# Attention and gated feed-forward on one core: bias tiles of head pairs two to four loaded ahead, first input split one step later

## The chip, the core and the metric

The kernel runs on one core of one Trainium2 chip. The metric is the device time of one execution in microseconds (us); lower is better. Several executions are timed and their median counts; one more execution is recorded by the hardware profiler, and all durations below come from that one.

The core has five engines with an instruction stream each: PE (matrix multiplies, with its weight loads shown apart as PEld), DVE (vector work), ACT (activations and copies), POOL (GpSimd, vector work here), and SP, which in this kernel only issues DMA transfers. The streams run on their own and wait for each other through semaphores.

## What is computed

```
scores = q k^T / 8 + bias[h, i, j]            # 4 batches, 8 heads, 576 x 576
bias   = relu(x[i, j] * w1 + b1) @ w2         # x = log1p(|i - j|) / log1p(max(i, 1)), hidden size 32
attn   = exp(scores - max) / sum
y      = attn v                               # to 4 x 576 x 512
h      = relu(y @ w_in)                       # 512 -> 1024
c      = three-tap convolution of h along the sequence
out    = (h * sigmoid(c)) @ w_out             # 1024 -> 512
```

The bias depends on the head and on the position, not on the batch. It is therefore computed once, written to device memory, and read back for each pair of heads.

## The kernel before

The program has three stages. The first computes the bias with small matrix multiplies and writes its rows to a buffer `bias_d` in device memory through five staging tiles; one of the staging tiles (`st34`) lives in the pool `raw_p`, which has two buffers of 9,728 bytes per partition. Attention starts underneath, and is the second stage. The third stage is the feed-forward network, batch after batch.

Attention is cut into 16 sequence steps `n`, each one pair of heads `p` of one batch `b`, in the order `seq = [(p, b) ...]`: pair 0 has `n` 0 to 3, pair 1 has 4 to 7, pair 2 has 8 to 11 and pair 3 has 12 to 15. A step has five units `t`: unit 0 holds the first 64 query rows of both heads, units 1 to 4 hold 128 rows of each head. The order is written out by hand: the list `flat` of 77 units, and one loop over it. In the iteration of unit `u` stand

- the score matrix multiplies (L350) of unit `u + 2` and their evaluation on DVE (`reduce`, L361): one instruction for each head, which adds the bias tile to the scores and takes the row's extreme;
- the exponentials (`expo`, L375, ACT) of unit `u + 1`;
- the transposes of unit `u` (L409, L421) and their copies on DVE and ACT (L91, L88);
- a few products with `v` (L458), which stand in the queue `fill`;
- a step of the preparation of the feed-forward weights (L97 and L103 on DVE, L99 on ACT, L131 and L132 on POOL).

`reduce` for unit `(n, t)` reads the bias tile `biast[p, t]`. A tile is 128 rows of both heads, 576 KB in two DMAs of 288 KB (L177); unit 0 has a smaller one (L179). The pool `bias_p` holds four tiles, one for each of `t` = 1 to 4, and `bias0_p` one for `t` = 0. The four batches of a pair use the same five tiles. The tiles of pair `p + 1` are loaded in the last batch of pair `p`: right behind the evaluation of unit `(n, t)`, which was the last to read the tile of pair `p`, its buffer is filled anew,

```
if b2 == B - 1 and p2 + 1 < NP:
    load_bias(p2 + 1, t2)
```

and read one step, five units, later. All these transfers stand in SP's stream, in the order in which the program issues them, among the queries and keys of step `n + 2` (L151, L152), the values of step `n + 1` (L166 to L169), the weights (L118), and the row sums' way through device memory (L484 to L486 and L491). The DMAs of SP count on eight semaphores in turn, and one that reuses a semaphore waits until the DMA before it on that semaphore has landed.

At the end of attention the result of batch 0 is split into two parts for the feed-forward multiplies: `x_parts(0, c)` for the four chunks `c`, two instructions each on POOL (L131, L132). Two chunks share one tile `xs` of the pool `raw_p`. Chunks 0, 1 and 2 stand in step 14 at units 2, 3 and 4, chunk 3 in step 15 at unit 0. The feed-forward multiplies of batch 0 (L523) begin in step 15 at unit 3. POOL also multiplies by the inverse sums (`apply_norm`, L498) in the same stream. When the four splits are done, a buffer of `x_p` becomes free, and the last weight rows (`raw_o`) are loaded into it.

Of the kernel before, what the change touches and what calls it, by code (L numbers as in the profile page):

```python
# [9 lines left out]
F32 = mybir.dt.float32  # L10
# [9 lines left out]
def attention_ffn_kernel(  # L20
# [12 lines left out]
    B, S, DM = out.shape  # L33
    NP = qk.shape[1]
# [4 lines left out]
    P = 128  # L39
# [19 lines left out]
    def pool(stack, name, bufs, **kw):  # L59
        return stack.enter_context(tc.tile_pool(name=name, bufs=bufs, reuse_waits="tile", **kw))  # L60
# [7 lines left out]
    raw_p = pool(ctx, "raw", 2)  # L68
# [15 lines left out]
    NSEQ = len(seq)  # L84
# [45 lines left out]
    def split_x(dst, x):  # L130
        first = nc.gpsimd.tensor_scalar(dst[:, 0], x, 1.0, 0.0, op0=ALU.mult, op1=ALU.add)  # L131
        nc.gpsimd.tensor_sub(dst[:, 1], x, dst[:, 0].bitcast(F32))  # L132
        return first

    with tc.manual_schedule():
# [3 lines left out]
        bias_p = pool(att, "bias", 4)  # L139
        bias0_p = pool(att, "bias0", 1)  # L140

        vts, qks, sms, biast = {}, {}, {}, {}


        def load(n):
# [23 lines left out]
            nc.sync.dma_start(vt[TL:P, 9], v[b, p, TL:P, 4])  # L169

        def load_bias(p, t):
            bt = bias_p.tile([P, 2, S], F32, name="bt") if t else bias0_p.tile([P, 1, S], F32, name="bt0")
            for h in range(2):
                c = (2 * p + h) * BW
                if t:
                    i0 = TL + (t - 1) * P
                    nc.sync.dma_start(bt[:, h], bias_rows[i0:i0 + P, c:c + S])  # L177
                else:
                    nc.sync.dma_start(bt[TL * h:TL * h + TL, 0, :], bias_rows[0:TL, c:c + S])  # L179
            biast[p, t] = bt  # L180
# [146 lines left out]
        def turned_sp(n, t):  # L327
            tile = sp_p.tile([P, 2 * S + 2], F32R, name="sr", tag=spt[n, t][1])
            nc.scalar.activation(tile[:, 2 * S:], pars[:, 0:2], AF.Copy)
            spt[n, t] = (tile, None)  # L330
# [28 lines left out]
        def reduce(ps, n, t, h):  # L359
            bt = biast[seq[n][0], t]  # L360
            nc.vector.tensor_tensor_reduce(  # L361
                out=halves(spt[n, t][0][:, h]),
                in0=ps[:, :, 0:HS],
                in1=halves(bt[:, h]),
                op0=ALU.add,
                op1=ALU.min,
                scale=-scale,
                scalar=3.0e38,
                accum_out=nms[n, t][:, h:h + 1],
            )  # L370

        def expo(n, t, h):
            sp, nm = spt[n, t][0], nms[n, t]
            col = 4 * h + t - 1 if t else 8
            exps[n, t, h] = nc.scalar.activation(  # L375
                sp[:, h], sp[:, h], AF.Exp, bias=nm[:, h:h + 1], scale=-1.0,
                accum_out=sms[n][:, col:col + 1],
            )
# [92 lines left out]
        def invert(n):  # L471
            sm, r = sms.pop(n), rr_t[n % 2][:, 0:9]
            nc.vector.tensor_scalar(r, sm, 1e-9, None, op0=ALU.add)
            nc.vector.reciprocal(r, r)
# [20 lines left out]
        def apply_norm(n):  # L495
            p, b = seq[n]
            assert waiting[n] == 0
            nc.gpsimd.tensor_mul(xb[b][:, p], xb[b][:, p], rbs.pop(n))  # L498
# [7 lines left out]
        def x_parts(b, c):  # L506
            if c % 2 == 0:
                xss["raw"] = raw_p.tile([P, 2, 2, S], F32R, name="xs", tag="raw")
            xs = xss["raw"][:, c % 2]
            first = split_x(xs, xb[b][:, c])  # L510
            if b == 1 and c == 0:
                tc.add_manual_dep(first.ins, gated[0, FC - 2].ins.name, mybir.DependencyInfo(
                    mybir.DependencyClass.Sync, mybir.DependencyReason.DATA))
            xss[b, c] = xs
# [57 lines left out]
        def heads(t):  # L572
            return (0, 1) if t else (0,)
# [25 lines left out]
        for i in range(NBLK):  # L599
# [18 lines left out]
            if fill:  # L618
                fill.popleft()()
        bias_out(*last)  # L620
        load_bias(0, 4)
        while fill:
            fill.popleft()()
        for _ in unit:
            pass
        for u in range(2):
            for h in heads(flat[u][1]):
                reduce(scores(*flat[u], h), *flat[u], h)
            if u == 0:
                for h in heads(flat[0][1]):  # L630
                    expo(*flat[0], h)
                turned_sp(*flat[0])
        pv_share = (2, 2, 1, 3, 2)
        hs_ff = {}
        raw_w = {}
# [4 lines left out]
        for u, (n, t) in enumerate(flat):  # L640
            p, b = seq[n]
            ui = units.index(t)
# [48 lines left out]
            if u + 2 < NU:  # L691
                n2, t2 = flat[u + 2]
                p2, b2 = seq[n2]
                if b2 == B - 1 and p2 + 1 < NP:
                    load_bias(p2 + 1, t2)
            if ui == (0 if n > 1 else 1) and n > 0:
                invert(n - 1)
            if ui == (2 if n > 1 else 3) and 1 <= n and n + 1 < NSEQ:
# [7 lines left out]

            if ui == 2 and n > 1:
                apply_norm(n - 2)
            if n == NSEQ - 2 and ui > 1:
                x_parts(0, ui - 2)  # L710
            if n == NSEQ - 1 and ui == 0:
                x_parts(0, 3)
            if n == NSEQ - 1 and ui in (1, 2):
                load_wo(FE - 1 + ui)
        while fill:
# [88 lines left out]
        for i, (b, f) in enumerate(steps):  # L804
# [14 lines left out]
            for c in range(KC):  # L819
# [5 lines left out]
                lambda f, gi, t=t: gs[b, f][:, gi, t * P:(t + 1) * P] for t in range(NT)  # L825
# [98 lines left out]
```

## Time and profile before

| | |
|---|---|
| median of 3 runs | 497.93 us (497.84 to 499.85) |
| the profiled execution | 498.59 us, of which the span from the first to the last instruction is 496.8 us |
| PE busy | 479.2 us, 96% of the span |
| DVE busy | 382.6 us, 77% |
| ACT busy | 310.3 us, 62% |
| POOL busy | 102.2 us, 21% |
| moved by DMA | 60.83 MB, mean 122 GB/s |
| TensorE clock granted | full in every slice |

Busy time tells little of a stage, since it is an average over three stages with different limits. The chain that ended last is followed back from the last instruction: at each step to what released it, or to the instruction before it on its engine. Where the same instruction group returns once for each step `n`, the distance between two of its starts is the time of one step.

### The profile page before, as it was taken

The page shows a single profiled execution, that of the slowest core. Times are in us where ns is not written, and L with a number is a line of the kernel's source. Part 1 is how long each engine was busy: PE and PEld are TensorE (multiplying, and loading weights), DVE is VectorE, ACT ScalarE, POOL GpSimd, SP SyncE. Part 2 cuts the span into 40 slices and gives each one's busy share as a digit, 9 for nine tenths or more (in the row PEclk, how much of TensorE's full clock was granted, in tenths as well). Part 3 has the DMA queues.
Part 4 walks back from the last instruction along what each step waited for, and adds up shares of the span by engine and source line. Part 5 has one row for each costly group of instructions (what it writes and reads, how often), then busy time and mean ns, then how long its engine had stood idle before and what let it go on. Part 6 is the DMA issues. An engine that isn't in the chain of part 4 may idle for free.

```text
span 496.8 us, 11125 instructions
## 1 busy us (share of the span) xinstructions
PE 479.2 (96%) x4202; PEld 352.5 (71%) x4202; DVE 382.6 (77%) x875; ACT 310.3 (62%) x747; POOL 102.2 (21%) x121
## 2 busy tenths in 40 slices
PE   5988889999999999999999999999999999999997
PEld 3333346666666666666666679989988899899986
DVE  6999957879898989889798919953896179928930
ACT  5888867778888887888788727722532144214520
POOL 1000000103332313333335513242072004400000
PEclk9999999999999999999999999999999999999999
DMA  5779646379877877789563300002000200020011
GB/s 137 270 248 325 229 160 168 92 216 245 188 169 191 237 194 163 196 235 250 157 186 85 110 25 26 1 1 86 0 1 0 107 1 1 1 85 1 1 43 63
DMA packets 32793, 60.83 MB, mean 122 GB/s; under 512 B 5580, under 2 KB 12260, under 8 KB 32740
## 3 DMA queue, kind: packets, MB, share of 16 engines
q1 hardware_dynamic: 32356, 59.78, 42.3%
q8 instruction: 33, 0.54, 0.5%
q10 hardware_dynamic: 384, 0.35, 0.2%
q14 instruction: 20, 0.16, 0.2%
HBM read 44.12 MB, written 15.98 MB: 121 GB/s over the span
## 4 chain that ended last, share of the span: by engine, by line
PE 87%; ACT 4%; DMA 4%; DVE 3%; issue 1%; SPq 0%; DVEq 0%
PE s L523 21%; PE o L458 16%; PE tp L771 16%; PE s L350 14%; PE tp L421 9%; PE s L262 6%; PE o L771 4%; DMA bt<-bias_d 3%; ACT st L288 2%; ACT y L241 1%; PE s L409 1%; DVE sp L361 1%; DMA pars<-in_par_dram 1%; DVE y L245 1%; DMA bias_d<-st 1%
## 5 line engine op out<-in xcount | busy, mean ns | idle before, releaser
L361 DVE CUSTOM_DVE_ANT_0 sp<-s,bt 128x576 f32<-128x576 f32 x144 | 104.1, 754 | 31.6 <-PE s L350 14.3
L375 ACT ACTIVATE sp<-sp,nm 128x576 f32<-128x576 f32 x144 | 109.9, 766 | 1.5 <-DVE nm L361 1.4
L523 PEld LDWEIGHTS s<-xs,wi 128*128 128x128 f32 x768 | 102.8, 189 | 1.2 <-issue 0.5
L523 PE MATMUL s<-xs,wi 128*128 128x288 f32 x768 | 103.6, 296 | 0.0
L350 PE MATMUL s<-qk 64*128 64x288 f32 (+1 forms) x640 | 93.3, 431 | 2.7 <-DVE nm L361 1.8
L350 PEld LDWEIGHTS s<-qk 64*128 64x128 f32 (+1 forms) x640 | 47.0, 175 | 45.7 <-DVE nm L361 13.9
L771 PE MATMUL tp<-wo,g 128*128 128x512 f32 x288 | 70.7, 390 | 0.0
L421 PE MATMUL tp<-identr,sr 64*128 64x64 f32 x1184 | 64.3, 247 | 0.0
L771 PEld LDWEIGHTS tp<-wo,g 128*128 128x128 f32 x288 | 53.7, 188 | 11.7 <-DVE g L766 0.8
L421 PEld LDWEIGHTS tp<-identr,sr 64*128 64x128 f32 x1184 | 55.6, 136 | 5.7 <-issue 0.6
L746 DVE SCALAR_TENSOR_TENSOR cv<-h,cw,cv 128x575 f32<-128x575 f32 x64 | 56.4, 881 | 2.5 <-ACT cv L741 0.6
L535 ACT ACTIVATE h<-s 128x576 f32<-128x576 f32 x32 | 20.9, 652 | 55.4 <-PE s L523 55.3
L458 PE MATMUL o<-ptx,vt 128*64 128x320 f32 x320 | 50.4, 442 | 1.2 <-ACT ptx L88 0.9
L262 PE MATMUL s<-y,pars 128*32 128x512 f32 (+8 forms) x352 | 46.2, 499 | 5.3 <-ACT st L288 2.2
L498 POOL TENSOR_TENSOR x<-x,rb 128x576 f32<-128x576 f32 x16 | 23.2, 1453 | 132.1 <-DMA rb<-r_d 131.2
L245 DVE TENSOR_SCALAR y<-tl,inv,nb 128x512 f32<-128x512 f32 (+8 forms) x116 | 49.9, 508 | 0.1
L458 PE MATMUL o<-pty,vt 128*64 128x256 f32 x320 | 44.2, 393 | 0.0
L262 PEld LDWEIGHTS s<-y,pars 128*32 128x32 f32 x352 | 16.0, 112 | 33.2 <-DVE y L245 16.8
L752 ACT ACTIVATE cv<-cv 128x576 f32<-128x576 f32 x32 | 21.7, 680 | 23.5 <-DVE cv L746 23.5
L753 DVE SCALAR_TENSOR_TENSOR cv<-cv,h 128x576 f32<-128x576 f32 x32 | 29.0, 907 | 5.5 <-ACT cv L752 5.5
L91 DVE COPY ptx<-tp 128x256 f32<-128x256 f32 (+1 forms) x64 | 32.0, 500 | 1.4 <-PE tp L421 1.2
L131 POOL TENSOR_SCALAR xs<-x 128x576 fp32r<-128x576 f32 x16 | 15.2, 950 | 81.4 <-PE s L523 66.6
(75 smaller groups left out, 567.3 us busy)
## 6 DMA issues: line engine op xcount, KB each, us to landing
qk<-in_qk_dram SPq DMA_DIRECT2D x32, 320.0 KB
bt<-bias_d SPq DMA_DIRECT2D x32, 288.0 KB
bias_d<-st SPq DMA_DIRECT2D x14, 607.0 KB
qk<-in_qk_dram SPq DMA_DIRECT2D x32, 144.0 KB
rb<-r_d SPq DMA_DIRECT2D x32, 144.0 KB
raw_w<-in_moe_w_in_dram SPq DMA_DIRECT2D x16, 256.0 KB
out_dram<-o SPq DMA_DIRECT2D x16, 256.0 KB
raw_w<-in_moe_w_out_dram SPq DMA_DIRECT2D x12, 256.0 KB
```

The source lines that it names most:

```text
L91: nc.vector.tensor_copy(o, i)
L245: nc.vector.tensor_scalar(y, dist[:, 0:n], inv[:, ig:ig + 1], nb1, op0=ALU.mult, op1=ALU.max)
L262: nc.tensor.matmul(ps[32 * j:32 * j + 32, a // 512 if n > 512 else blk % 2, 0:min(n - a, 512)], w2b, ys[j][:, a:min(n, a + 512)], start=Tr ...
L350: nc.tensor.matmul(ps[po, a, 0:HS], qt[rows, qo:qo + po.stop - po.start], qt[rows, KO + hh * HS:KO + hh * HS + HS], start=True, stop=True,)
L361: nc.vector.tensor_tensor_reduce(out=halves(spt[n, t][0][:, h]), in0=ps[:, :, 0:HS], in1=halves(bt[:, h]), op0=ALU.add, op1=ALU.min, scale ...
L375: exps[n, t, h] = nc.scalar.activation(sp[:, h], sp[:, h], AF.Exp, bias=nm[:, h:h + 1], scale=-1.0, accum_out=sms[n][:, col:col + 1],)
L421: tr = nc.tensor.transpose(ps[a][:, TL * s:TL * s + TL].bitcast(F32R), spf[ra, j:j + P], identr[ra, ra])
L458: nc.tensor.matmul(po[D * h:D * h + D, 0:width], vt[:, slot, :], pt[:, blk, :], start=(c == 0), stop=(c == 4),)
L523: nc.tensor.matmul(ps[:, a, 0:HS], wi[c][:, pw, cs], xss[b, c][:, px, a * HS:(a + 1) * HS], start=(i == 0), stop=(i == 3 * KC - 1),)
L746: nc.vector.scalar_tensor_tensor(out=cv[:, o:o + S - 1], in0=h[:, i:i + S - 1], scalar=cw[:, f, kk:kk + 1], in1=cv[:, o:o + S - 1], op0=AL ...
L753: nc.vector.scalar_tensor_tensor(out=cv, in0=cv, scalar=1.0, in1=h, op0=ALU.add, op1=ALU.mult)
L771: nc.tensor.matmul(ps, lhs(f, gi), wo[f][:, wj, cs], start=(f == 0 and i == 0), stop=(f == FC - 1 and i == 2),)
```

## The change

```diff
-        vts, qks, sms, biast = {}, {}, {}, {}
+        vts, qks, sms, biast, pairs = {}, {}, {}, {}, {}
...
         def load_bias(p, t):
-            bt = bias_p.tile([P, 2, S], F32, name="bt") if t else bias0_p.tile([P, 1, S], F32, name="bt0")
+            if t and (p == 1 or p == NP - 1 and t < 3):
+                if t % 2:
+                    pairs[p, t // 2] = raw_p.tile([P, 2, 2, S], F32, name="bt2", tag="raw")
+                bt = pairs[p, (t - 1) // 2][:, (t - 1) % 2]
+            else:
+                bt = bias_p.tile([P, 2, S], F32, name="bt") if t else bias0_p.tile([P, 1, S], F32, name="bt0")
...
+        ahead = {(1, 2): (1, 1), (2, 1): (1, 2), (2, 4): (1, 3), (3, 2): (1, 4)}
+        ahead.update({(B + b, 1): (2, b + 1) for b in range(B)})
+        ahead.update({(2 * B + b, 1): (NP - 1, b + 1) for b in range(2)})
...
-                if b2 == B - 1 and p2 + 1 < NP:
+                if b2 == B - 1 and p2 + 1 < NP and (p2 + 1, t2) not in biast:
                     load_bias(p2 + 1, t2)
+            if (n, ui) in ahead:
+                load_bias(*ahead[n, ui])
...
-            if n == NSEQ - 2 and ui > 1:
-                x_parts(0, ui - 2)
-            if n == NSEQ - 1 and ui == 0:
-                x_parts(0, 3)
+            if n == NSEQ - 2 and ui > 2:
+                x_parts(0, ui - 3)
+            if n == NSEQ - 1 and ui in (0, 1):
+                x_parts(0, ui + 2)
```

The table `ahead` names, by step and unit, a tile to load there. Pair 1's tiles 1 to 4 come in steps 1 to 3, into the two buffers of `raw_p`, two tiles in one buffer. Pair 2's tiles 1 to 4 come one in each of steps 4 to 7, into `bias_p`, whose four buffers are free once pair 0 is over. Pair 3's tiles 1 and 2 come in steps 8 and 9, into one buffer of `raw_p`; its tiles 3 and 4 and all tiles 0 are loaded where they were, but tiles 3 and 4 go into the buffers of pair 2's tiles 1 and 2. The four input splits move one unit back, to step 14 units 3 and 4 and step 15 units 0 and 1. All instructions on PE, DVE and ACT stay, in their order.

On SP, in step 11, where pair 3's tiles came in (`bt`: a bias tile; `bias_d`: the bias in device memory; a name with DMAHW is one of the eight semaphores of SP's DMAs, one with DVE or PE is that engine's), before, from the weights ahead of tile 2 to the values behind tile 4:

```order
L118 DMA raw_w<-in_moe_w_out_dram 128x512 [waits DMAHW2_49,DVE_49,Activation_49]
L177 DMA bt<-bias_d 128x576 [waits DVE_49]
L177 DMA bt<-bias_d 128x576
L177 DMA bt<-bias_d 128x576 [waits DVE_49]
L177 DMA bt<-bias_d 128x576 [waits DMAHW6_49]
L151 DMA qk<-in_qk_dram 64x1280 [waits DMAHW7_49,PE_49]
L152 DMA qk<-in_qk_dram 64x2x288 [waits DMAHW0_49]
L151 DMA qk<-in_qk_dram 64x1280 [waits DMAHW1_49]
L152 DMA qk<-in_qk_dram 64x2x288 [waits DMAHW2_49]
L118 DMA raw_w<-in_moe_w_out_dram 128x512 [waits DMAHW3_49,DVE_49,Activation_49]
L177 DMA bt<-bias_d 128x576 [waits DMAHW4_49,DVE_49]
L177 DMA bt<-bias_d 128x576 [waits DMAHW5_49]
```

and with the change:

```order
L118 DMA raw_w<-in_moe_w_out_dram 128x512 [waits DMAHW6_49,DVE_49,Activation_49]
L182 DMA bt<-bias_d 128x576 [waits DMAHW7_49]
L182 DMA bt<-bias_d 128x576 [waits DMAHW0_49]
L151 DMA qk<-in_qk_dram 64x1280 [waits PE_49]
L152 DMA qk<-in_qk_dram 64x2x288
L151 DMA qk<-in_qk_dram 64x1280
L152 DMA qk<-in_qk_dram 64x2x288 [waits DMAHW4_49]
L118 DMA raw_w<-in_moe_w_out_dram 128x512 [waits DMAHW5_49,DVE_49,Activation_49]
L182 DMA bt<-bias_d 128x576 [waits DMAHW6_49]
L182 DMA bt<-bias_d 128x576 [waits DMAHW7_49]
```

Tile 1 (ahead of this piece) and tile 2 are gone from the step, and the loads that are left wait for no DVE instruction any more.

On SP in step 3, unit 2, from the queries and keys of step 5 to the values of step 4, before:

```order
L151 DMA qk<-in_qk_dram 64x1280 [waits DMAHW7_49,PE_49]
L152 DMA qk<-in_qk_dram 64x2x288 [waits DMAHW0_49]
L151 DMA qk<-in_qk_dram 64x1280 [waits DMAHW1_49]
L152 DMA qk<-in_qk_dram 64x2x288 [waits DMAHW2_49]
L118 DMA raw_w<-in_moe_w_in_dram 128x512 [waits DMAHW3_49,DVE_49,Activation_49]
L177 DMA bt<-bias_d 128x576 [waits DMAHW4_49,DVE_49]
L177 DMA bt<-bias_d 128x576 [waits DMAHW5_49]
L166 DMA vt_106<-in_v_dram 64x576 [waits DMAHW6_49,PE_49]
```

and with the change:

```order
L151 DMA qk<-in_qk_dram 64x1280 [waits PE_49]
L152 DMA qk<-in_qk_dram 64x2x288
L151 DMA qk<-in_qk_dram 64x1280
L152 DMA qk<-in_qk_dram 64x2x288 [waits DMAHW2_49]
L118 DMA raw_w<-in_moe_w_in_dram 128x512 [waits DMAHW3_49,DVE_49,Activation_49]
L182 DMA bt_1288<-bias_d 128x576 [waits DMAHW4_49]
L182 DMA bt_1288<-bias_d 128x576 [waits DMAHW5_49]
L182 DMA bt_1288<-bias_d 128x576 [waits DMAHW6_49,DMAHW4_49]
L182 DMA bt_1288<-bias_d 128x576 [waits DMAHW7_49,DMAHW5_49]
L166 DMA vt_106<-in_v_dram 64x576 [waits DMAHW0_49,PE_49]
```

Pair 1's tile 4 stands there twice: the test `not in biast` comes ahead of the table's own entry `(3, 2)` in the same iteration. The second copy waits on DMAHW4 and DMAHW5, which the first copy's DMAs count on.

On POOL at the end of attention (`x_121`: the result of batch 0; `xs`: its split parts), before:

```order
L131 TENSOR_SCALAR xs<-x_121 128x576
L132 TENSOR_TENSOR xs<-x_121,xs 128x576 [waits Pool_49]
L131 TENSOR_SCALAR xs<-x_121 128x576
L132 TENSOR_TENSOR xs<-x_121,xs 128x576 [waits Pool_49]
L131 TENSOR_SCALAR xs<-x_121 128x576
L132 TENSOR_TENSOR xs<-x_121,xs 128x576 [waits Pool_49]
L131 TENSOR_SCALAR xs<-x_121 128x576
L132 TENSOR_TENSOR xs<-x_121,xs 128x576 [waits Pool_49]
```

and with the change:

```order
L131 TENSOR_SCALAR xs<-x_121 128x576
L132 TENSOR_TENSOR xs<-x_121,xs 128x576 [waits Pool_49]
L131 TENSOR_SCALAR xs<-x_121 128x576
L132 TENSOR_TENSOR xs<-x_121,xs 128x576 [waits Pool_49]
L131 TENSOR_SCALAR xs<-x_121 128x576 [waits DVE_49]
L132 TENSOR_TENSOR xs<-x_121,xs 128x576 [waits Pool_49]
L131 TENSOR_SCALAR xs<-x_121 128x576
L132 TENSOR_TENSOR xs<-x_121,xs 128x576 [waits Pool_49]
```

The order on POOL is as it was. The third split has a new wait for DVE: its tile takes the buffer that pair 3's tiles 1 and 2 hold until the evaluation of unit (15, 2).

## Rows read from the trace of the kernel before

**Rows 1.** The page: the span, and the busiest engine's share of it.

```profile
span 496.8 us, 11125 instructions
...
PE 479.2 (96%) x4202; PEld 352.5 (71%) x4202; DVE 382.6 (77%) x875; ACT 310.3 (62%) x747; POOL 102.2 (21%) x121
```

**Rows 2.** The chain that ended last, in order of time: start us, us, what.

```profile
69.26 4.11 DMA bt<-bias_d
...
112.86 1.76 PE o L458 x12
...
127.09 1.77 PE o L458 x12
...
155.55 1.77 PE o L458 x12
...
172.32 9.28 DMA bt<-bias_d
...
198.79 1.77 PE o L458 x12
...
227.24 1.77 PE o L458 x12
...
256.60 1.77 PE o L458 x12
```

**Rows 3.** Who waited for whom, whole span: waited us in total, times, longest us.

```profile
DVE sp L361 <- DMA bt<-bias_d: 3.4, 3, 1.6
```

**Rows 4.** DVE in order of time: start us, us, instruction [idle before <-what ended it].

```profile
123.83 0.76 DVE L361 CUSTOM_DVE_ANT_0 sp<-s,bt 128x576 f32<-128x576 f32 x1
...
181.74 0.76 DVE L361 CUSTOM_DVE_ANT_0 sp<-s,bt 128x576 f32<-128x576 f32 x1 [1.10 <-DMA bt<-bias_d]
...
239.75 0.76 DVE L361 CUSTOM_DVE_ANT_0 sp<-s,bt 128x576 f32<-128x576 f32 x1 [1.64 <-DMA bt<-bias_d]
```

**Rows 5.** SP's issues in order of time: start us, us, DMA, count.

```profile
114.04 1.67 SPq L177 DMA_DIRECT2D bt<-bias_d  x2
...
222.78 2.60 SPq L177 DMA_DIRECT2D bt<-bias_d  x4
...
229.84 2.13 SPq L177 DMA_DIRECT2D bt<-bias_d  x2
...
278.69 0.83 SPq L118 DMA_DIRECT2D raw_o<-in_moe_w_out_dram  x2
```

**Rows 6.** Stretches of step 11: engines' busy us, TensorE clock, DMA busy share, GB/s.

```profile
219.00:222.00 3.00, 3.00 (x46) 2.19 (x41) 2.89 (x10) 2.97 (x10) 0.66 (x2) 1.00 0.60 171
...
225.00:228.00 3.00, 3.00 (x41) 1.75 (x40) 3.00 (x10) 2.87 (x9) 0.96 (x2) 1.00 0.94 288
...
231.00:234.00 3.00, 3.00 (x30) 1.86 (x28) 2.59 (x8) 2.32 (x6) 1.13 (x2) 1.00 1.03 206
```

**Rows 7.** POOL at the end of attention, in order of time.

```profile
274.37 0.67 POOL L131 TENSOR_SCALAR xs<-x 128x576 fp32r<-128x576 f32 x1
275.12 1.41 POOL L132 TENSOR_TENSOR xs<-x,xs 128x576 fp32r<-128x576 f32 x1
...
277.25 1.41 POOL L132 TENSOR_TENSOR xs<-x,xs 128x576 fp32r<-128x576 f32 x1
278.63 1.41 POOL L498 TENSOR_TENSOR x<-x,rb 128x576 f32<-128x576 f32 x1
```

**Rows 8.** DVE: L473 elsewhere, then the end of attention, in order of time.

```profile
163.63 0.17 DVE L473 TENSOR_SCALAR rr<-sm 128x9 f32<-128x9 f32 x1
...
275.59 1.02 DVE L97 TENSOR_SCALAR w<-cwr 24x128 int32<-24x128 int32 x1
...
277.91 0.74 DVE L361 CUSTOM_DVE_ANT_0 sp<-s,bt 128x576 f32<-128x576 f32 x1
...
279.26 0.81 DVE L473 TENSOR_SCALAR rr<-sm 128x9 f32<-128x9 f32 x1
```

**Rows 9.** PE: the first feed-forward multiplies, in order of time.

```profile
286.90 3.45 PE L523 MATMUL s<-xs,wi 128*128 128x288 f32 x24
```

## The prediction, on record before the changed kernel ran

> **What bounds the kernel now.** The page comes first: PE is busy for 96% of the 496.8 us, and DVE is next with 77% [rows 1]. So time can only be won where PE stands still or is held back. The second view is the chain of waits in order of time. The first products with v of a step, twelve matrix multiplies of L458, return in it once for each step n, and the distances between their starts are a ruler [rows 2]. From 112.86 to 127.09 is one step, 14.23 us; from 127.09 to 155.55 are two, 28.46, which is 14.23 each. From 198.79 to 227.24 are two again, 28.45. Two stretches are longer. From 155.55 to 198.79 are three steps in 43.24, and three clean ones would be 42.69: 0.55 lost. From 227.24 to 256.60 are two in 29.36 against 28.46: 0.90 lost. The first long stretch holds the passage from pair 1 to pair 2, the second that from pair 2 to pair 3.
>
> The third view says what they lost it to. Over the whole span DVE waited three times for a bias tile, 3.4 us in all [rows 3]. Two of these waits stand in the two long stretches: 1.10 us ahead of the evaluation at 181.74 and 1.64 us ahead of that at 239.75 [rows 4]. Both are unit 4 of a pair's first step, the tile that is issued last. The third wait is what is left of the 3.4, about 0.7 us; it belongs to pair 0 at the end of the bias stage, where a load issued at 69.26 took 4.11 us [rows 2], and no line of the change touches it. PE lost less than DVE waited, 0.55 of 1.10 and 0.90 of 1.64, so about 0.55 to 0.74 us of each wait are taken up by work that PE has in hand. The passage from pair 0 to pair 1 costs nothing: its unit 4 at 123.83 shows no wait [rows 4], and its step takes the clean 14.23.
>
> Why the tiles are late is in SP's issues and the stretches of step 11. Tiles 2 and 3 are issued at 222.78 and tile 4 not before 229.84 [rows 5]. Ahead of the pile the DMA engines are busy 0.60 of the time, then 0.94 and 1.03, at 288 and 206 GB/s [rows 6]. The tile lands just ahead of 239.75, 9.9 us after its issue; that of pair 2 took 9.28 us [rows 2]. An unhindered one, at 69.26, took 4.11.
>
> **The change, part by part.**
>
> Pair 2's tiles 1 to 4 leave step 7 and come one by one in steps 4 to 7. The last of them is issued in step 7 at unit 1, ahead of the queries that it stood behind, and is read in the next step's unit 4. The whole 1.10 us of DVE's wait goes, and PE gets back 0.55.
>
> Pair 3's tiles 1 and 2, four DMAs of 288 KB, leave step 11; tiles 3 and 4 stay. Tile 4 is issued where it was, or some tenths earlier, since its buffer no longer waits for DVE. What stood ahead of it is smaller by 1,152 KB, but the tile is only 1.64 us late. At the two rates of the full stretch, 288 and 206 GB/s, 1,152 KB are 4.0 to 5.6 us; tile 1's half was mostly through before the queue filled (share 0.60), so I count tile 2 alone: 576 KB, 2.0 to 2.8 us. That is more than 1.64. The wait goes, with 0.4 to 1.2 us to spare, and PE gets back 0.90.
>
> Pair 1's tiles 1 to 4 leave step 3 and come in steps 1 to 3. There was no wait to remove: 0. They could delay queries, values or weights of steps 1 to 3, but none is read earlier than the bias was, and step 3's load falls by three tiles.
>
> Pair 1's tile 4 is loaded twice, the second copy behind the landing of the first: 576 KB more, and SP stands still in between. Behind SP stand the values of step 4, the row sums of step 3 and the next weights. The evaluation at 123.83 now needs the second copy. From both sides: the first is issued about 114.04 [rows 5] and takes 4.11 to 9.28 us, the two ends of the rows; so does the second. It lands between 122.3 and 132.6, which is 1.6 us early to 8.8 us late; PE would pay up to 8.8 − 0.6 = 8.2. I take nothing, by the row at 69.26, which it is nearest to: the two tiles in front (1,152 KB) that made the queue long are gone from this step. The values of step 4 then follow about 119 and land within the same 4.11 by 123.2, ahead of their first use at 127.09.
>
> Nothing is put ahead of the first evaluations of step 1, and DVE and ACT keep their instructions. The slices of `raw_p` are read by the same L361 of 0.76 us.
>
> The input split: POOL's order stays, and one wait is added. The third split began at 274.37 [rows 7]; now it waits until the evaluation that begins at 277.91 has ended [rows 8], about 278.6, 4.2 us later. Queued behind it on POOL are its second instruction, the fourth split and an `apply_norm`, which end about 284.3 instead of 280.0. The first feed-forward multiplies start at 286.90 [rows 9], and need the third and fourth chunk later than the first two: at least 4 us are left. The load of `raw_o`, now at 278.69 [rows 5], waits for the fourth split and moves to about 283; the row sums of step 14 come just behind it. Their `apply_norm` is for batch 2, which is read much later. 0 for the moved split.
>
> Here a rule can be weighed. The row first: L473, a DVE instruction of 0.17 us elsewhere, took 0.81 at 279.26 and ended with the `apply_norm` that POOL had begun at 278.63; L97 took 1.02 at 275.59 in the same way behind the L132 of 275.12 [rows 7, 8]. The moved split keeps POOL busy beside L473, with an L132 of 1.41 instead; the extra is at most 1.41 − (0.81 − 0.17) = 0.77 us on DVE, and L97's 1.02 falls, as POOL is then waiting. I take 0.
>
> The Trainium skill's page "SBUF — State Buffer", section "Who interferes with whom", says why: GpSimd shares one pair of ports with DVE as an exclusive lock, and whoever comes second is blocked for the whole instruction. By that rule the sum would be up to 0.77 us worse; the rows agree that the lock exists.
>
> **The sum.** 0.55 + 0.90 = 1.45 us. The profiled execution takes 498.59 (span 496.8), and becomes 497.14 (span 495.35). The median of the runs, 497.93, lies 0.66 below the profiled one; against it the forecast is 496.48, say 496.5, 0.29% less.
>
> **The rivals.**
>
> A smaller gain: in unprofiled runs the waits are shorter, or a remainder of pair 3's wait stays. For it: the median is 0.66 us below the profiled execution, and the waits are the sort of thing that differs. Against: the profiled tiles were late by two different amounts with the same cause. Worked out: 1.45 − 0.66 = 0.79 of gain, 497.1; with only pair 2's wait gone 0.55, 497.4.
>
> Nothing: the loads still pile up, or DMA work just moves its lateness to another tile. For it: queries, values and weights keep loading in every step. Against: steps without bias loads run at 14.23 throughout. 497.9.
>
> The port: the moved split blocks DVE's L473, and DVE hands it to PE in full, 0.77: 497.25. For it [rows 7, 8]; against it that L97's block of 0.85 vanishes a little earlier. It is the skill's rule above as a mechanism of this kernel.
>
> Slower: pair 1's second copy of tile 4 comes late. Its place is DVE ahead of unit (4, 4). For it: SP's stream waits out a whole landing, and tile 4 of the other pairs took over 9 us. Against: the shorter queue. If the first copy takes 9.28 and the second 4.11, it lands at 127.4, 3.6 late, and PE pays 3.0: 497.93 − 1.45 + 3.0 = 499.5; with 9.28 twice 8.2, 504.7. It makes the kernel slower than before when the second copy lands later than 123.83 + 0.6 + 1.45 = 125.9.
>
> **How the numbers follow.** Forecast 0.66, smaller gain 0.14, nothing 0.07, port 0.05, slower 0.08. A measurement of this kernel can tell about 0.5% from no change, 2.5 us: below 495.4 or above 500.4. For over 0.5% faster both waits would have to be worth their full DVE length, 2.74 us, 495.2: 0.05, from the forecast's own tail. For over 0.5% slower the upper half of the slow rival: 0.04. The range takes in the forecast, the smaller gain, the port and nearly all of "nothing": 495.4 to 498.3. It leaves out the slow rival and the tail.
>
> **What would show it.** In the profile afterwards DVE's evaluation waits only once for a bias tile, at the end of the bias stage, for about 0.7 us; the ruler shows 14.23 in the steps to pair 2 and pair 3; SP shows four bias DMAs in step 3 with a standstill between the second and the third, and evaluation (4, 4) without idle time; POOL waits some 4 us ahead of the third split; the first L523 comes 1.45 us earlier, about 285.4. It is wrong if a step is still over 14.3, if DVE waits at (4, 4) or behind L473, if L523 waits for POOL, or if the feed-forward stage changes length.

## Result: slower by 1.15%, and the profile after

The changed kernel takes 503.74 us (median of 9 executions, 501.16 to 505.29), the kernel before beside it 497.84 (9 executions, 496.39 to 500.37). The ratio is 1.0115, interval 1.0097 to 1.0133: slower. The prediction said 496.5, with 498.3 as the upper end. A ratio is worked out apart from the medians, here and below, and leaves out executions more than 1.5% above the fastest of their kernel, so it need not be the quotient of two medians.

The profiled execution took 501.16 us, the shortest of the nine, so its trace shows less than half of the loss. The page of the changed kernel, its span and engines:

```profile
span 499.4 us, 11114 instructions
...
PE 480.0 (96%) x4202; PEld 353.9 (71%) x4202; DVE 377.7 (76%) x875; ACT 310.6 (62%) x747; POOL 101.9 (20%) x121
```

PE's instructions are as many as in [rows 1]; it is busy for 480.0 us against 479.2. Of the 2.6 us more of span, 1.8 are PE standing still. The lines have moved by five: L361 is L366 now, L458 is L463, L177 and L179 are L182 and L184, L491 is L496, L473 is L478, L498 is L503, L523 is L528.

The chain of waits in order of time (start us, us, what), which holds the ruler of [rows 2]:

```profile
127.44 1.77 PE o L463 x12
141.67 1.76 PE o L463 x12
156.65 1.77 PE o L463 x12
170.90 1.77 PE o L463 x12
177.02 8.41 DMA raw_w<-in_moe_w_in_dram
187.54 1.91 PE o L463 x12
201.92 1.77 PE o L463 x12
216.14 1.76 PE o L463 x12
233.96 6.60 DMA raw_w<-in_moe_w_out_dram
240.59 2.88 DMA r_d<-rt
245.15 1.84 PE o L463 x12
```

I number a step of the ruler by the mark at which it ends: step 4 ends at 127.44. Step 5 is clean, 14.23. Step 6 has 14.98, step 8 has 16.64. From 216.14 to 245.15 are steps 11 and 12, 29.01 against 28.46. The chain now runs through a DMA in three places, and none is the tile 4 that was late before: they are weights (`raw_w`) and row sums.

DVE in order of time shows the greatest new wait, and the view of who waited for whom its sum:

```profile
172.86 0.76 DVE L366 CUSTOM_DVE_ANT_0 sp<-s,bt 128x576 f32<-128x576 f32 x1 [2.35 <-DMA bt<-bias_d]
```

```profile
DVE sp L366 <- DMA bt<-bias_d: 3.3, 3, 2.4
```

Three waits and 3.3 us again, as in [rows 3], but the greatest is at another place: 172.86 is the evaluation for unit 0 of pair 2. Behind it PE stands still for 0.63 us, ahead of 173.98. In the same step PE stands still for 1.30 us more ahead of 187.54, where ACT's exponentials come late behind the weights of 177.02. Both the weights and tile 0 are issued by lines that the change does not touch. SP's issues (start us, us, DMA, count) say why tile 0 is late:

```profile
113.58 7.08 SPq L182 DMA_DIRECT2D bt<-bias_d  x4
120.75 0.47 SPq L166 DMA_DIRECT2D vt<-in_v_dram  x1
...
125.75 1.13 SPq L496 DMA_DIRECT2D rb<-r_d  x2
...
140.85 1.13 SPq L496 DMA_DIRECT2D rb<-r_d  x2
...
156.64 1.13 SPq L496 DMA_DIRECT2D rb<-r_d  x2
...
166.54 1.91 SPq L184 DMA_DIRECT2D bt<-bias_d  x2
...
171.59 1.12 SPq L496 DMA_DIRECT2D rb<-r_d  x2
```

The four loads of pair 1's tile 4 in step 3 take 7.08 us of SP's stream, where two take 0.90: the second copy waits for the first to land (asked for the stretch from 114.5 us on, the view has its two DMAs start at 119.64, and nothing before them). Then SP needs 15.1, 15.8 and 15.0 us from one inverse-sum load (`rb`) to the next. Tile 0 goes out at 166.54. In the kernel before, the same view had:

```profile
124.92 1.27 SPq L491 DMA_DIRECT2D rb<-r_d  x2
137.85 1.12 SPq L491 DMA_DIRECT2D rb<-r_d  x2
150.28 1.13 SPq L491 DMA_DIRECT2D rb<-r_d  x2
...
159.26 1.67 SPq L179 DMA_DIRECT2D bt<-bias_d  x2
...
163.80 1.12 SPq L491 DMA_DIRECT2D rb<-r_d  x2
```

There the same three intervals are 12.9, 12.4 and 13.5 us, less than a step's 14.23, and tile 0 goes out 7.3 us earlier.

### The profile page after: what moved, and what is told of

It reads as the page before. It is cut to its first block, busy times and chain, and to the rows that moved or that the text cites. A ratio compares the mean times of both kernels' runs of the same rounds, so it can differ in the third digit from the quotient of the medians.

```text
span 499.4 us, 11114 instructions
## 1 busy us (share of the span) xinstructions
PE 480.0 (96%) x4202; PEld 353.9 (71%) x4202; DVE 377.7 (76%) x875; ACT 310.6 (62%) x747; POOL 101.9 (20%) x121
## 4 chain that ended last, share of the span: by engine, by line
PE 85%; DMA 6%; ACT 4%; DVE 2%; issue 1%; SPq 1%; DVEq 0%; ACTq 0%
PE s L528 21%; PE o L463 16%; PE tp L781 15%; PE s L355 14%; PE tp L426 8%; PE s L267 6%; PE o L781 4%; ACT st L293 2%; DMA raw_w<-in_moe_w_in_dram 2%; DMA raw_w<-in_moe_w_out_dram 1%; DMA pars<-in_par_dram 1%; DMA bt<-bias_d 1%; PE s L414 1%; ACT y L246 1%; ACT sp L380 1%
## 5 line engine op out<-in xcount | busy, mean ns | idle before, releaser
L366 DVE CUSTOM_DVE_ANT_0 sp<-s,bt 128x576 f32<-128x576 f32 x144 | 104.1, 754 | 38.3 <-PE s L355 16.9
L528 PEld LDWEIGHTS s<-xs,wi 128*128 128x128 f32 x768 | 102.8, 189 | 1.2 <-issue 0.5
L528 PE MATMUL s<-xs,wi 128*128 128x288 f32 x768 | 103.5, 296 | 0.0
L355 PEld LDWEIGHTS s<-qk 64*128 64x128 f32 (+1 forms) x640 | 47.4, 175 | 45.7 <-DVE nm L366 11.7
L503 POOL TENSOR_TENSOR x<-x,rb 128x576 f32<-128x576 f32 x16 | 22.9, 1432 | 152.1 <-DMA rb<-r_d 136.8
L463 PE MATMUL o<-ptx,vt 128*64 128x320 f32 x320 | 50.4, 443 | 2.7 <-ACT sp L380 1.8
L463 PE MATMUL o<-pty,vt 128*64 128x256 f32 x320 | 44.3, 393 | 0.0
L267 PEld LDWEIGHTS s<-y,pars 128*32 128x32 f32 x352 | 16.6, 114 | 32.6 <-DVE y L250 17.2
L762 ACT ACTIVATE cv<-cv 128x576 f32<-128x576 f32 x32 | 21.8, 680 | 23.6 <-DVE cv L756 23.6
L131 POOL TENSOR_SCALAR xs<-x 128x576 fp32r<-128x576 f32 x16 | 15.2, 949 | 85.1 <-PE s L528 66.5
```

Of the source, the lines that this page charges most:

```text
L267: nc.tensor.matmul(ps[32 * j:32 * j + 32, a // 512 if n > 512 else blk % 2, 0:min(n - a, 512)], w2b, ys[j][:, a:min(n, a + 512)], start=Tr ...
L355: nc.tensor.matmul(ps[po, a, 0:HS], qt[rows, qo:qo + po.stop - po.start], qt[rows, KO + hh * HS:KO + hh * HS + HS], start=True, stop=True,)
L366: nc.vector.tensor_tensor_reduce(out=halves(spt[n, t][0][:, h]), in0=ps[:, :, 0:HS], in1=halves(bt[:, h]), op0=ALU.add, op1=ALU.min, scale ...
L463: nc.tensor.matmul(po[D * h:D * h + D, 0:width], vt[:, slot, :], pt[:, blk, :], start=(c == 0), stop=(c == 4),)
L528: nc.tensor.matmul(ps[:, a, 0:HS], wi[c][:, pw, cs], xss[b, c][:, px, a * HS:(a + 1) * HS], start=(i == 0), stop=(i == 3 * KC - 1),)
```

## The experiments

Each ratio is to the kernel before on the same chip; the interval is in brackets. Each version ran four or ten times. Two theories of the loss stood first: the second copy's standstill on SP, and the tile more that each of steps 4 to 7 carries. The moved split (by one unit, not by a step as the title has it) was the third. Marks of the ruler that the chain does not show are read from PE in order of time, where they lie up to 0.1 us earlier.

**Without the second copy.**

```diff
-            if (n, ui) in ahead:
+            if ahead.get((n, ui), (0, 0)) not in biast:
                 load_bias(*ahead[n, ui])
```

> The change without the second copy of pair 1's tile 4; all else as changed. Theory 'stream' (one tile more in every step makes SP's stream of a step longer than the step's 14.23 us, and the lag adds up over steps 4 to 7): one of five added tiles falls, so a part comes back, 500.5 to 502.5 us. Rival 'double' (the standstill between the two copies is what puts SP behind): all of the loss comes back, 496.5 to 498. Rival 'split' (the moved input split costs): no change, 503 to 504.

498.19 us, 1.0011 [0.9983, 1.0038]. Nearly all of the loss goes with the second copy. In its profile every step of the ruler up to 14 has 14.23, DVE waits for a bias tile only once after the bias stage (0.34 us at 238.44), and yet it is not faster than before. SP's inverse-sum loads in steps 3 to 7 of that run:

```profile
120.36 1.13 SPq L496 DMA_DIRECT2D rb<-r_d  x2
...
135.35 1.50 SPq L496 DMA_DIRECT2D rb<-r_d  x2
...
150.82 1.13 SPq L496 DMA_DIRECT2D rb<-r_d  x2
...
166.46 1.12 SPq L496 DMA_DIRECT2D rb<-r_d  x2
```

They too lie 15.0 to 15.6 us apart, but start 5.4 us earlier than in the changed kernel.

**The kernel before with the moved split alone.**

```diff
-            if n == NSEQ - 2 and ui > 1:
-                x_parts(0, ui - 2)
-            if n == NSEQ - 1 and ui == 0:
-                x_parts(0, 3)
+            if n == NSEQ - 2 and ui > 2:
+                x_parts(0, ui - 3)
+            if n == NSEQ - 1 and ui in (0, 1):
+                x_parts(0, ui + 2)
```

> The kernel before with the input split moved one unit back and nothing else. 'Stream' and 'double': as before, 497.8 within half a per cent. 'Split': 502 to 504.

497.11 us, 1.0005 [0.9979, 1.0030]: no cost of the split can be seen. The run shows more than it was made for. Its bias loads are those of before, and in its profile DVE waits for none of them at the passages (0.6 us in two are left, at the end of the bias stage); no step is long there. So the two long waits of [rows 4] are not in every execution.

**Tiles that nobody reads.** The kernel before, with four more loads of 576 KB at unit 1 of steps 4 to 7, into the free buffers of `raw_p`:

```diff
+        def extra(b):
+            if b % 2 == 0:
+                spare.append(raw_p.tile([P, 2, 2, S], F32, name="spare", tag="raw"))
+            for h in range(2):
+                c = (4 + h) * BW
+                nc.sync.dma_start(spare[-1][:, b % 2, h], bias_rows[TL + b * P:TL + b * P + P, c:c + S])
...
+            if p == 1 and ui == 1:
+                extra(b)
```

> The kernel before, all its loads where they were, plus four bias tiles of 576 KB that nobody reads, one at unit 1 of each of steps 4 to 7, where the change has pair 2's. 'Stream': slower than the change itself, since step 7 keeps its five tiles too, 503 to 508; the DMAs of the inverse sums (L491) of steps 4 to 7 are issued over 15 us apart. 'Double' and 'split': as before, 497.8 within half a per cent.

511.07 us, 1.0244 [1.0161, 1.0328], more than the 503 to 508 expected. Nobody waits for these loads, and by the medians they cost 13.7 us. Who waited for whom, in that run:

```profile
DVE sp L361 <- DMA bt<-bias_d: 13.3, 4, 7.0
ACT wu L99 <- DMA raw_w<-in_moe_w_in_dram: 5.1, 2, 4.4
```

What stands behind them in SP's stream is late: the `rb` loads are 15.2 to 21.8 us apart in steps 4 to 7, and step 8 takes 25.17 us. A tile more in each of these steps is more than the stream has room for here, where step 7 keeps its own five tiles as well and nothing was loaded ahead in steps 1 to 3.

**A lean version.** The kernel before, the later split, and only tile 1 of pairs 2 and 3 ahead, in steps 5 and 9:

```diff
-            bt = bias_p.tile([P, 2, S], F32, name="bt") if t else bias0_p.tile([P, 1, S], F32, name="bt0")
+            if t == 1 and p > 1:
+                if p == 2:
+                    pairs[0] = raw_p.tile([P, 2, 2, S], F32, name="bt2", tag="raw")
+                bt = pairs[0][:, p - 2]
+            else:
+                bt = bias_p.tile([P, 2, S], F32, name="bt") if t else bias0_p.tile([P, 1, S], F32, name="bt0")
...
+        ahead = {(5, 1): (2, 1), (9, 1): (3, 1)}
...
```

> The kernel before with one tile each of pairs 2 and 3 loaded ahead (tile 1, in steps 5 and 9, into one buffer of the staging pool), the split one unit later, no second copy. 'Stream': steps 5 and 9 run late by a little and recover in the next, both waits of DVE go, 495.5 to 497.5. 'Double': about the same, 496.5. 'Split': 502 to 504.

500.60 us, 1.0041 [1.0005, 1.0078]: a miss. Tile 4 of pair 2 still comes late (bias waits of 4.5 us in four, the longest, 2.94 us, for this tile). Taking the first tile out of the pile did not bring the last one forward: it goes out at 174.34, before at 172.32.

**The bytes without the standstill.** The second copy goes into a free buffer of `bias_p` that nobody reads.

```diff
         def load_bias(p, t):
-            if t and (p == 1 or p == NP - 1 and t < 3):
+            if (p, t) == (1, 4) and (p, t) in biast:
+                bt = bias_p.tile([P, 2, S], F32, name="bt")
+            elif t and (p == 1 or p == NP - 1 and t < 3):
...
-            biast[p, t] = bt
+            biast.setdefault((p, t), bt)
```

> The changed kernel, but the second copy of pair 1's tile 4 goes into a bias buffer that is free and is read by nobody: the same 576 KB are moved, by the same number of DMAs at the same place in SP's stream, and nothing stands still between the two copies. Theory 'standstill' (the wait of the second copy for the first one's landing sets SP back some 5 us, and with a tile more in each of steps 4 to 7 it can't catch up before tile 0 of pair 2 is due): about as without the second copy, 496.5 to 499.5 us, no step over 14.5 us, DVE waits for no bias tile of pair 2. Rival 'bytes' (576 KB more at this place fill the DMA engines): as the changed kernel, 501.2 to 505.3, steps 6 and 8 at about 15.0 and 16.7.

502.16 us, 1.0074 [1.0043, 1.0104]. The ratio lies between those without the second copy and with it, so the 496.5 to 499.5 of the theory "standstill" was missed: the loads cost something without the wait. The profiled execution was the shortest of its ten, so the same kernel ran once more:

> Once more the second copy into a buffer that nobody reads, for the profile of another execution: the first one profiled took 497.78 us, the shortest of its ten (497.8 to 507.4). Theory 'stream': the two DMAs more make SP's stream in steps 3 to 8 longer, and the longer executions lose their time where a tile of the next pair or a weight tile comes late: steps 6 to 9 at 15 to 18 us, DVE waiting for bt or raw_w; 499 to 505 us. Rival: the loss lies outside the attention stage (last multiply of the feed-forward stage later, with steps all at 14.23).

501.32 us, 1.0056 [1.0036, 1.0076]. This profile has steps 8 and 9 at 17.02 and 15.93, ACT waits 3.2 us for a weight tile and DVE 2.3 for a bias tile: the theory's places. Step 12 has 15.86.

**The standstill without the bytes.** The second load brings 16 columns of each half and waits for the first all the same.

```diff
-            if (n, ui) in ahead:
+            if ahead.get((n, ui), (0, 0)) not in biast:
                 load_bias(*ahead[n, ui])
+            if (n, ui) == (3, 2):
+                for h in range(2):
+                    nc.sync.dma_start(biast[1, 4][:, h, 0:16],
+                        bias_rows[TL + 3 * P:S, (2 + h) * BW:(2 + h) * BW + 16])
```

> The changed kernel without the second copy's bytes but with its standstill: the second load of pair 1's tile 4 brings only 16 columns of each half (16 KB instead of 576), which have to wait for the first copy's landing all the same. Theory 'standstill' (SP's 5 us of standing still are the cost): near the changed kernel, 501 to 505 us, tile 0 of pair 2 late. Rival 'bytes' (576 KB more in step 3 are the cost, as the copy to an unread buffer hinted with 502.2): as without the second copy, 496.5 to 499.5, since the small copy lands 2 to 3 us after the first. If both count, in between: 499.5 to 501.

504.34 us, 1.0136 [1.0106, 1.0167]: with 16 KB it loses as much as the changed kernel. SP in that run, around the two loads:

```profile
113.22 0.90 SPq L182 DMA_DIRECT2D bt<-bias_d  x2
119.25 1.01 SPq L708 DMA_DIRECT2D bt<-bias_d  x2
120.36 0.47 SPq L166 DMA_DIRECT2D vt<-in_v_dram  x1
```

Between 114.12 and 119.25 SP issues nothing, 5.1 us. So the wait, with two small DMAs, is enough for the whole loss. The 576 KB without the wait (the version before this one) cost about half.

**The changed kernel again**, for a profile nearer to its median:

> The changed kernel once more, for the profile of a second execution: the first one profiled took 501.16 us, the shortest of its nine, and its 2.6 us over before leave half of the median's loss unseen. In it the second copy of pair 1's tile 4 landed just in time for unit 4 of step 4. Theory 'both': in longer executions that copy lands after the evaluation is due, DVE waits there for bt by up to 3 us (as in the kernel before with the second copy alone), PE's granted clock falls to 0.50 for some 3 us, step 4 takes 15 to 17 us and the passage to pair 2 is late as before; 503 to 505 us. Rival 'passage only': step 4 stays at 14.23 and all that is lost lies in steps 6 to 8 and 12.

504.34 us, 1.0135 [1.0103, 1.0167]; the profiled execution took 503.68. Theory "both" falls and "passage only" is nearly right: at unit 4 of step 4 DVE does not wait, and what is lost lies in steps 6 to 12. The chain of waits in this execution:

```profile
126.73 1.77 PE o L463 x12
...
147.13 8.27 DMA vt<-in_v_dram
155.54 1.92 PE o L463 x12
...
162.63 7.93 DMA qk<-in_qk_dram
...
173.19 3.40 PE o L463 x12
...
189.42 1.77 PE o L463 x12
```

Values are late at 155.54, queries and keys at 170.57; step 7 has 17.65 and step 8 has 16.23. Who stood still, PE for the queries and then DVE for tile 0:

```profile
170.70 1.23 PE L355 MATMUL s<-qk 64*64 64x288 f32 x6 [1.64 <-DMA qk<-in_qk_dram]
```

```profile
174.15 0.76 DVE L366 CUSTOM_DVE_ANT_0 sp<-s,bt 128x576 f32<-128x576 f32 x1 [4.61 <-DMA bt<-bias_d]
```

The stretches of this time (us; busy PE, PEld, DVE, ACT, POOL; granted clock; DMA share; GB/s) show a second cost:

```profile
160.00:168.00 8.00, 8.00 (x94) 5.60 (x92) 7.03 (x21) 7.22 (x22) 3.65 (x5) 1.00 0.91 220
168.00:171.00 3.00, 1.36 (x9) 0.52 (x8) 1.54 (x6) 2.59 (x7) 1.13 (x2) 0.91 1.00 218
171.00:177.00 6.00, 6.00 (x38) 2.92 (x34) 1.77 (x5) 2.00 (x5) 0.00 (x0) 0.50 0.47 114
```

PE is busy for 1.36 of 3 us, and then its granted clock stands at 0.50, the lower of its two levels (1.2 instead of 2.4 GHz), for 6 us. The twelve products at 173.19 take 3.40 us instead of 1.77. PE is busy all the while, also in the 3 us of DVE's wait that fall into this stretch, and stays slow for some 3 us after the wait has ended at 174.15. In the first profiled execution, 501.16 us, the clock was full in every slice; over its other eight executions the mean granted clock was 0.993 to 0.997. So executions of one kernel differ in this, too; how much of the 4 us between them it makes was not measured.

**The second copy alone**, in the kernel before, right behind the first load:

```diff
                     nc.sync.dma_start(bt[:, h], bias_rows[i0:i0 + P, c:c + S])
...
+            if (p, t) == (1, 4):
+                for h in range(2):
+                    c = (2 * p + h) * BW
+                    nc.sync.dma_start(bt[:, h], bias_rows[TL + 3 * P:S, c:c + S])
             biast[p, t] = bt
```

> The kernel before, with one addition: pair 1's tile 4 is loaded a second time into the same buffer, right behind the first load in step 3. The standstill is there, but the bias tiles of pairs 2 and 3 are loaded at their old places, so steps 4 to 6 carry no tile more. Theory 'standstill alone': the step ahead of pair 2 loses as in the changed kernel, 501 to 505 us. Theory 'standstill and spreading together': the steps of before needed 12.4 to 13.5 us of SP where they carried no bias tile, against 14.23 of the step, so 5 us are caught up in about four steps, by step 7; 497 to 499.5, and one step between 4 and 6 is long by 1.5 us at most. The slow rival of the prediction (the second copy itself late at unit 4 of step 4): DVE waits there for bt, up to 3 us.

502.88 us, 1.0114 [1.0091, 1.0137]. The 497 to 499.5 of the theory that standstill and spread act together was missed. Here it is the slow rival of the prediction: in the kernel before, pair 1's other tiles are in front, and the copy is late for unit 4 of step 4. DVE, and the stretches behind it:

```profile
124.87 0.76 DVE L365 CUSTOM_DVE_ANT_0 sp<-s,bt 128x576 f32<-128x576 f32 x1 [1.53 <-DMA bt<-bias_d]
```

```profile
127.00:130.00 3.00, 0.80 (x13) 0.49 (x11) 2.30 (x7) 1.46 (x4) 0.00 (x0) 0.95 0.25 62
130.00:133.00 3.00, 3.00 (x14) 1.32 (x10) 1.46 (x5) 1.16 (x4) 0.00 (x0) 0.50 0.74 191
```

Steps 4 and 5 have 17.16 and 15.87, the clock falls again; steps 6 to 11 are clean. So what this version lost by the second copy it lost at another place than the changed kernel. Step 12, the passage to pair 3, has 15.87 as well.

**Another queue.** The changed kernel with pair 2's tiles issued by ACT:

```diff
-                    nc.sync.dma_start(bt[:, h], bias_rows[i0:i0 + P, c:c + S])
+                    (nc.scalar if p == 2 else nc.sync).dma_start(bt[:, h], bias_rows[i0:i0 + P, c:c + S])
```

> The changed kernel, second copy included, but pair 2's tiles are issued on ACT's DMA queue instead of SP's. The bytes and the moments of steps 4 to 7 stay. Theory 'stream' (SP's in-order issue with few DMAs in flight is what is too long with a tile more in each step): 496.5 to 499, no step over 14.5 us, tile 0 of pair 2 in time. Rival 'DMA engines' (the bytes of these steps are too many, whichever queue issues them): 501 to 505, the same long steps 6 and 8. A third way: ACT itself is held up by issuing eight DMAs; then PE waits for ACT in steps 4 to 7, some tenths each.

499.33 us, 1.0028 [1.0001, 1.0055]. The same bytes, the standstill included, and steps 6 to 14 are clean. Steps 4 and 5 have 16.24 and 15.61. What is left is the third way of the expectation: ACT itself is held up, once, at its first issue behind the standstill.

```profile
123.95 1.61 ACTq L182 DMA_DIRECT2D bt<-bias_d  x2
125.61 0.78 ACT L380 ACTIVATE sp<-sp,nm 128x576 f32<-128x576 f32 x1 [2.78 <-DVE rt L91]
```

The view names DVE as what ended ACT's 2.78 us, but ACT's own issue runs until 125.56, and PE then waits 1.11 us for ACT at 127.29. Why the issue did not start before 123.95 no run shows.

The Trainium skill, page "DMA: Bandwidth & Descriptors", section "Issuing engines are not separate DMA queues", says that transfers of all issuing engines share the same 16 DMA engines, so that a second issuer only saves the time that a sequencer spends on issuing, usually little. No run here shows the sharing by itself. On the saving the measurement differs: two loads of a tile take 0.90 us of SP's stream, and without them the first two intervals between its `rb` loads behind step 3 are 12.4 and 13.5 us, where the changed kernel had 15.1 and 15.8.

With the second copy gone too and all tiles ahead on ACT's queue (the same line, with `(p, t) in ahead.values()` in place of `p == 2`):

> The changed kernel without the second copy, and all tiles that are loaded ahead on ACT's DMA queue; SP's stream is then shorter in every step than in the kernel before. If SP's stream is what keeps the version without the second copy from being faster than before, this one is: 495.5 to 497, every step 14.23, last one 13.86. If PE has nothing to get back there in ordinary executions (as the version with the later split alone suggested), 497 to 498.5. If issuing on ACT costs something, some tenths in each of steps 1 to 9, up to 500.

500.10 us, 1.0038 [1.0002, 1.0075]: no gain, and rather a loss. The profiled execution (497.11) shows one step of 14.84; what the longer ones lost to isn't in it.

**Without the spread.** The changed kernel with pair 2's tiles at their old place:

```diff
-        ahead.update({(B + b, 1): (2, b + 1) for b in range(B)})
```

> The changed kernel, second copy and standstill included, but pair 2's tiles 1 to 4 are loaded at their old place in step 7, so that steps 4 to 6 carry no tile more. Theory 'standstill and spreading together' (SP, set back in step 3, can't catch up while each step carries a tile more): SP catches up in steps 4 to 6, no weight or query tile comes late, and at the passage to pair 2 at most the 0.55 us of before are lost; 497 to 499 us. Rival 'the second copy alone': it lands after unit 4 of step 4 is due, as in the kernel before with the second copy added; step 4 at 16 to 17 us with PE's clock at 0.50, 500 to 503 us. Rival 'the pile': five tiles in step 7 and SP late from before, DVE waits in step 8 for longer than 1.1 us; 499 to 502.

499.44 us, 1.0037 [1.0007, 1.0067]. The theory's 497 to 499 was missed by little. And without the second copy as well:

> As the run beside it, and without the second copy: pair 1's tiles ahead once each, pair 2's at their old place, pair 3's tiles 1 and 2 ahead, later split. Nothing sets SP back in step 3, steps 4 to 6 carry no tile more. Theory 'stream': the least loaded stream of all versions with tiles ahead; 496.5 to 498, steps at 14.23 but for the passage to pair 2, up to 14.8; the spread-out version without the second copy took 498.19, this one is some tenths to 1 us better. Rival: the spread of pair 2 costs nothing by itself, and both are the same within 0.3%.

498.62 us, 1.0027 [0.9997, 1.0057]. In the first of the two the ruler's steps 4 to 7 are clean: SP catches up, with 12.6, 12.3 and 14.1 us between the inverse-sum loads, and tile 0 goes out at 158.71. Its profiled execution, 503.36, was the longest of its ten, and lost at the passages: steps 8 and 12 have 16.12 and 16.42, and DVE waits 2.53 and 2.74 us for a bias tile there. In step 7 that is the rival "the pile" of the expectation; in step 11 two of the five tiles had been loaded ahead.

The four cases beside each other:

| ratio to before | pair 2 spread over steps 4 to 7 | pair 2 in step 7 |
|---|---|---|
| second copy | 1.0115 and 1.0135 | 1.0037 |
| no second copy | 1.0011 | 1.0027 |

The copy costs 1.0 to 1.2% with the spread and 0.1% without it, where the two intervals overlap. With pair 1's tiles ahead, neither is dear alone; together they are. (The copy alone in the kernel before, at 1.0114, lost its time otherwise, as shown above.) SP's stream in the profiled executions, by its `rb` load at the end of step 3 and the issue of pair 2's tile 0, goes with the ratio where the spread is in SP's stream (the first execution of the copy to another buffer was the shortest of its ten, and says little of its median):

| | `rb` at | tile 0 at | ratio |
|---|---|---|---|
| spread, no second copy | 120.36 | 161.16 | 1.0011 |
| spread, copy to another buffer (two executions) | 122.74, 123.28 | 161.26, 165.48 | 1.0074, 1.0056 |
| spread, standstill with 16 KB | 125.36 | 166.28 | 1.0136 |
| the changed kernel (two executions) | 125.75, 124.64 | 166.54, 168.17 | 1.0115, 1.0135 |
| no spread, second copy | 124.28 | 158.71 | 1.0037 |
| before | 124.92 | 159.26 | 1 |

No version was faster than before.

## Why the prediction was wrong

**The step that failed: what the spread and the second copy cost on SP, two terms that were put at nothing.** Where 1.45 us less were forecast, 5.90 more were measured. "Pair 2's tiles 1 to 4 leave step 7 and come one by one in steps 4 to 7" was followed by what they gain, and not by what SP does with them. SP issues in order, and a transfer waits for a semaphore that an earlier one must give back by landing. A step without bias tiles took 12.4 to 13.5 us of that stream; with a tile it took 15.0 to 15.8 in the changed kernel and, without the copy, 15.0 to 15.6 (120.36, 135.35, 150.82 and 166.46), and PE's step has 14.23. A lead of 0.7 to 1.8 us a step becomes a lag of 0.7 to 1.6. Where SP is ahead, such an interval holds its own waiting as well (11.7, 13.7 and 16.6 us in the run with neither spread nor copy), so those of the changed kernel, where SP is behind, weigh most. The rows were there to sum: the kernel before shows the intervals between its `rb` loads. The argument "steps without bias loads run at 14.23 throughout" spoke for the other side: they did, because SP had room in them.

The spread alone can be borne, since loading pair 1 ahead gives SP a lead of 4.6 us (120.36 against 124.92) that the steps then use up. The second copy takes that lead away before the steps begin (125.75). I had written that "SP stands still in between", and named what stands behind it, but followed only the tile's own landing and that of the values. The price was one of order: about 5 us of SP for every transfer behind it, with no room to catch up. Its two loads alone, without the wait, set SP back by 2.4 and 2.9 us (122.74 and 123.28 against 120.36).

**The slow rival** had 0.08 and a time of 499.5 to 504.7, which holds the result by luck. Its place was wrong: the second copy is in time for unit 4 of step 4 in both profiles of the changed kernel. It is right for the second copy alone in the kernel before.

**The gain of 1.45 us** was of one execution. The run with the moved split alone has the same bias loads and neither of the two waits, and the version that loses no time to bias tiles (all steps up to 14 at 14.23) measures 1.0011. The smaller-gain rival said that such waits differ between executions; they can be nothing.

Pair 3's share, 0.90, had a fault of its own besides. Tile 4 was to go out at its old moment or some tenths earlier, with 2.0 to 2.8 us less in front of it. Without the second copy it goes out 3.90 us behind the mark of step 11 (230.25 and 226.35), where before it was 2.60 (229.84 and 227.24), and DVE still waits 0.34 us for it. In the second profile of the changed kernel it waits 1.69, as much as before.

**What was right.** The wait of POOL, and the port. POOL in order of time, and DVE at the end of attention, in the changed kernel:

```profile
280.99 0.67 POOL L131 TENSOR_SCALAR xs<-x 128x576 fp32r<-128x576 f32 x1 [3.74 <-DVE nm L366]
```

```profile
278.44 0.20 DVE L97 TENSOR_SCALAR w<-cwr 24x128 int32<-24x128 int32 x1
...
281.51 0.18 DVE L478 TENSOR_SCALAR rr<-sm 128x9 f32<-128x9 f32 x1
```

POOL waits 3.74 us ahead of the third split (predicted about 4), L97 falls from 1.02 to 0.20, as POOL stands still beside it, and L478 from 0.81 to 0.18 [rows 8]: it does not collide after all. The last step of the ruler has 13.85 where it had 14.37, about half a microsecond that I had not counted; the later split alone, with no bias tile in `raw_p` for POOL to wait for, still had 14.39. The standstill between the second and the third of four DMAs is there. No L528 waits for POOL: in the chain the first begins at 289.31, and began at 286.97 before (PE in order of time has 286.90 for it, [rows 9]): 2.34 us later instead of 1.45 earlier. From there to the end of the span are 210.1 us, against 209.8 before. So nearly all of the profiled execution's loss lies ahead of it, in attention.

**Open.** Whether what limits SP's stream is its eight semaphores or the order alone: no run changed their number. Whether the versions at 1.0028 to 1.0041 lose anything real: their intervals end close to 1. What a quieter stream would give beyond before: nothing was found, since with the loads of before (the run with the moved split alone) PE's steps are already clean in an execution of 497.08 us.

## What to carry to other kernels

Sum the time of each in-order DMA queue per step, waits for free semaphores included, and set it beside the step of the engine that bounds; a transfer that nobody waits for takes its share of the queue from those that somebody does. When a table adds loads to places that a rule already serves, make sure that each tile is loaded once: a second write to the same buffer made the in-order queue stand here for a whole landing, 5.1 us. And before counting on a wait as a gain, look whether a second execution has it.

## What the runs showed that was not expected

Four unread tiles, 2.3 MB, cost 13.7 us by the medians, 3.4 us each, though no engine waited for them. And a stop of PE cost twice: after 1.36 busy us in 3, the clock was granted at 0.50 for 6 us, so that work already in hand ran at half speed; in two executions of one kernel, 501.16 and 503.68 us, one had this and the other had not.
